# The first block pass begun on the first head pair, batch 1's v load behind its k, and q's first rows as two transfers

## The chip, the cores and the metric

One core of a Trainium2 chip runs the kernel. The metric is the device time of one execution in microseconds (us). Before the change three runs gave 291.13, 292.02 and 292.19 us: a median of 292.02 us.

## The reference

Eight batches of eight heads, 576 rows of 64 elements, go through a linear attention. Its output, as 4608 tokens of 512 features, goes through two matmuls with a leaky ReLU between them.

```python
q_s = q - np.max(q, axis=-1, keepdims=True)       # softmax of each q row
q_s = np.exp(q_s)
q_s = q_s / (np.sum(q_s, axis=-1, keepdims=True) + 1e-09)
k_s = k - np.max(k, axis=2, keepdims=True)        # softmax of k over the rows
k_s = np.exp(k_s)
k_s = k_s / (np.sum(k_s, axis=2, keepdims=True) + 1e-09)
kv = np.einsum('bhsd,bhse->bhde', k_s, v)
attn = np.einsum('bhsd,bhde->bhse', q_s, kv)
x = attn.transpose(0, 2, 1, 3).reshape(4608, 512)
h = x @ w_in                                      # 512 x 2048
out = np.maximum(0.01 * h, h) @ w_out             # 2048 x 512
```

## The kernel before, in words

The order of each engine's instructions is the order in which the program writes them; nothing is rescheduled. Work of a later batch is put between the matmuls of an earlier token tile by hand: `at(t, u, ...)` hangs functions on unit `u` of token tile `t`, and `run(t, u)` calls them (lines 493 to 500). Tile 0 has units 0 to 31 for `layer1` (two halves of 256 tokens, 16 blocks each) and 32 to 47 for `layer2`.

**Layout.** A batch's q, k or v is one tile of 128 partitions x 4 x 9 x 64: a head has 64 partitions, so a partition half holds one of two heads, four such pairs lie side by side, and a partition holds nine rows. `load` (line 72) issues such a tile on SyncE's queue, cut into pieces by head pair and by row.

**The start, batch 0.** SyncE issues rows 0 to 3 of q (`RA`), k in two halves, v in two halves, and the other q rows (lines 91 to 98). Then, engine by engine:

- VectorE takes the maxima of the first q rows (`q_first`, line 236) and ScalarE makes 16 exps with sums from them (line 241). VectorE makes k's maxima (`k_tree`, line 163), which TensorE turns and spreads (lines 338 and 353), and subtracts them (`k_sub_ps`, line 364). ScalarE exponentiates k (`k_exp`, line 204) and casts v to bf16 (`v_cast`, line 214).
- TensorE multiplies k and v for two of the four head pairs (`kv_pair`, line 373). VectorE scales the product to `kd` (lines 384 and 389). TensorE transposes q (`q_transpose`, line 397), the result is copied out (`q_keep`, lines 413 and 415), and `attend` (lines 421 and 431) multiplies it with `kd` and writes `xT`, the input of `layer1`. Rows 4 and 5 (`R1`) and 6 to 8 (`R2`) of q follow by `q_max` (228), `q_sub` (259, on GpSimd), `q_exp` (267), `q_sum` (276 and 278) and `q_norm` (283).
- `wake` (line 327) are matmuls on zeros whose result nobody reads.

**The first block pass.** `layer1` multiplies one 128-column block `j` of `w_in` with four feature blocks of `xT`; `part` says which of the four. Blocks 0 to 7 are begun with the two feature blocks of the first `attend` (lines 654 to 658) in four PSUM banks and ended with the other two (line 669); blocks 8 to 15 are done in one go. The transposes of q's rows 4 to 8 hang on units 7 and 11, their `attend` on unit 13. The PSUM pool of these results has six banks.

**Weights.** GpSimd's queue loads them, casting fp32 to bf16. `load_w_in(j0, j1)` (line 130) is four transfers over blocks `j0` to `j1`: two groups of feature blocks, and for each the two partition halves. The calls are for blocks 0 to 7, 8 to 11 and 12 to 15, the first two behind a tiny copy into `gate` that waits for a piece of k (lines 519 and 545), the third behind GpSimd's subtraction of q rows 4 and 5. `w_out` comes in six transfers behind a third such copy, which waits for batch 1's k (line 581).

**Batch 1.** Its loads stand in SyncE's queue behind a transfer of 256 bytes into `held`, whose source is a piece of `w_in_sb`, so that they are issued only when that piece has landed:

```python
hold_sync(0, w_in_sb[0:1, 1, 11 * P : 12 * P])
st[1]["k"] = load(k, 1, "k_raw", [(H0, ALLR), (H1, ALLR)])
st[1]["q"] = load(q, 1, "q_raw", [(ALLH, ALLR)])
st[1]["v"] = load(v, 1, "v_raw", [(ALLH, ALLR)])
nc.gpsimd.tensor_copy(out=gate[:, 0:1], in_=st[1]["k"][:, 0, 0, 0:1])
```

Partition 0 of feature block 1 is written by the third of the four transfers of `load_w_in(8, 12)`. Batch 1's softmax work hangs on units 15, 31, 34, 39 and 43, and its `attend_x` on 47. From token tile 1 on the plan is not touched by the change.

Of the kernel before, what the change touches and what calls it, by code (L numbers as in the profile page):

```python
# [8 lines left out]
FP32 = mybir.dt.float32  # L9
# [11 lines left out]
R = 9  # L21
HL = 4
# [3 lines left out]
def kernel(  # L26
# [9 lines left out]
    nc = tc.nc  # L36
# [3 lines left out]
    B, H, S, D = q.shape  # L40
    C = H * D
    T = B * S
    Cm, F = moe_w_in.shape
# [3 lines left out]
    P = 128  # L47
    NB = C // P
    NF = F // P
# [19 lines left out]
    BANK_TAG = "bank2k"  # L69


    def load(src, b, name, cuts):

        t = raw_pool.tile([P, HL, R, D], FP32, name=name, tag="raw")
        flat = src[b].rearrange("h s d -> (h s d)").rearrange(
            "(hl p r d) -> p hl r d", hl=HL, p=P, r=R
        )
        for hs, rs in cuts:
            nc.sync.dma_start(
                out=t[:, hs, rs].rearrange("p h r d -> p h (r d)"),  # L80
                in_=flat[:, hs, rs].rearrange("p h r d -> p h (r d)"),
            )
        return t

    ALLH, ALLR = slice(0, HL), slice(0, R)
# [2 lines left out]
    st = [{} for _ in range(B)]  # L88


    st[0]["q"] = load(q, 0, "q_raw", [(ALLH, RA)])
    st[0]["k"] = load(k, 0, "k_raw", [(slice(0, 2), ALLR), (slice(2, 4), ALLR)])
    st[0]["v"] = load(v, 0, "v_raw", [(slice(0, 2), ALLR), (slice(2, 4), ALLR)])
    qflat = q[0].rearrange("h s d -> (h s d)").rearrange("(hl p r d) -> p hl r d", hl=HL, p=P, r=R)
# [35 lines left out]
    def load_w_in(j0, j1):  # L130
        fs = slice(j0 * P, j1 * P)
        for gg in range(2):
            for hp in range(2):
                nc.gpsimd.dma_start(  # L134
                    out=w_in_t[hp * D : (hp + 1) * D, gg, :, fs], in_=w_in_r[gg, hp, :, :, fs]
                )
# [3 lines left out]
    def load_w_out(js):  # L140
        nc.gpsimd.dma_start(out=w_out_sb[:, js, :], in_=w_out_r[:, js, :])  # L141
# [61 lines left out]
    def k_exp(b, hs):  # L203
        nc.scalar.activation(  # L204
            out=st[b]["ke"][:, :, hs].rearrange("p r h d -> p h r d"),
            in_=st[b]["k"][:, hs],
            func=AF.Exp,
        )

    def v_cast(eng, b, gg):  # L210
        o = vb2[b % 2][:, :, gg, 0:128].rearrange("p r (h d) -> p h r d", h=2)
        i = st[b]["v"][:, 2 * gg : 2 * gg + 2]
        if eng is nc.scalar:
            eng.copy(out=o, in_=i)
        else:
            eng.tensor_copy(out=o, in_=i)  # L216
# [8 lines left out]
    def q_max(b, rs):  # L225
        n = rs.stop - rs.start
        st[b]["qmax", rs.start] = m = small_pool.tile([P, HL, n], FP32, name="qmax")
        nc.vector.tensor_reduce(out=m, in_=st[b]["q"][:, :, rs], axis=AX.X, op=ALU.max)  # L228
# [27 lines left out]
    def q_sub(eng, b, rs):  # L256
        n = rs.stop - rs.start
        qs = st[b]["q"][:, :, rs]
        eng.tensor_tensor(  # L259
            out=qs,  # L260
            in0=qs,
            in1=st[b]["qmax", rs.start].unsqueeze(3).to_broadcast([P, HL, n, D]),
            op=ALU.subtract,
        )

    def q_exp(b, rs):
        nc.scalar.activation(  # L267
            out=st[b]["qe"][:, rs].rearrange("p r h d -> p h r d"),
            in_=st[b]["q"][:, :, rs],
            func=AF.Exp,  # L270
        )

    def q_sum(b, rs):
        n = rs.stop - rs.start
        qsum = small_pool.tile([P, n, HL], FP32, name="qsum")
        nc.vector.reduce_sum(out=qsum, in_=st[b]["qe"][:, rs], axis=AX.X)  # L276
        st[b]["qrec", rs.start] = qrec = small_pool.tile([P, n, HL], FP32, name="qrec")
        nc.vector.reciprocal(out=qrec, in_=qsum)
# [46 lines left out]
    def wake(n):  # L325
        for i in range(n):
            nc.tensor.matmul(  # L327
                wake_ps, lhsT=zero[:, 0:P], rhs=zero, start=(i == 0), stop=(i == n - 1)
            )
# [16 lines left out]
    def k_all_dve(b, i):  # L346
        st[b]["kr", i] = kr = small_pool.tile([P, 2], FP32, name="kr")
        nc.vector.tensor_reduce(out=kr, in_=st[b]["kT", i], axis=AX.X, op=ALU.max)
# [19 lines left out]
    def kv_pair(b, gg):  # L368
        pkv = [psB_pool.tile([P, 130], FP32, name="pkv1", tag=BANK_TAG) for _ in range(2)]
        for r in range(R):  # L370
            for hh in range(2):
                rows = slice(hh * L, (hh + 1) * L)
                nc.tensor.matmul(
                    pkv[hh][:, 0:129],
                    lhsT=st[b]["ke"][rows, r, 2 * gg : 2 * gg + 2].rearrange("p h d -> p (h d)"),
                    rhs=vb2[b % 2][rows, r, gg, 0:129],
                    start=(r == 0),
                    stop=(r == R - 1),
                )
        st[b]["pkv", gg] = pkv  # L380
# [28 lines left out]
    def q_keep(eng, b, r0, n, ggs=(0, 1)):  # L409
        for gg in ggs:  # L410
            o, i = st[b]["qT", gg][:, :, r0 : r0 + n], st[b]["ps", r0][:, gg::2]
            if eng is nc.scalar:
                eng.copy(out=o, in_=i)
            else:
                eng.tensor_copy(out=o, in_=i)
# [77 lines left out]
    def at(t, u, *fns):  # L493
        while t > 0 and u >= 32:
            t, u = t + 1, u - 32
        hooks.setdefault((t, u), []).extend(fns)
# [11 lines left out]
        st[b]["v"] = load(v, b, "v_raw", whole)  # L508

    held = const_pool.tile([1, 2, 128], BF16)  # L510
    XR = (slice(0, 5), slice(5, R))

    def hold_sync(i, src):
        nc.sync.dma_start(out=held[:, i], in_=src)  # L514
# [19 lines left out]
    wake(1)  # L534
    k_sub_ps(0, 0, HA)
    k_exp(0, slice(0, 1))
    k_all_dve(0, 1)
    k_all_pe(0, 1)
    wake(5)
    k_sub_ps(0, 0, HB)  # L540
    k_exp(0, slice(1, 2))
    v_cast(nc.scalar, 0, 0)
    v_cast(nc.scalar, 0, 1)
    k_sub_ps(0, 1)
    nc.gpsimd.tensor_copy(out=gate[:, 0:1], in_=st[0]["k"][:, HL - 1, R - 1, D - 1 : D])  # L545
    load_w_in(8, 12)
    k_exp(0, slice(2, 3))
    q_first_rec(0, RA)
    q_norm(0, RA)
    kv_pair(0, 0)  # L550
    wake(1)
    q_transpose(0, 0, 4)
    wake(2)
    for hh in range(2):
        kd_rec(0, 0, hh)
        kd_one(nc.vector, 0, 0, hh)
    q_keep(nc.scalar, 0, 0, 4, (0,))
    k_exp(0, slice(3, 4))
    attend(0, [0, 2], 0, 256, nc.scalar)
    wake(1)  # L560
    kv_pair(0, 1)
    q_max(0, R1)
    q_sub(nc.gpsimd, 0, R1)
    load_w_in(12, 16)
    q_keep(nc.vector, 0, 0, 4, (1,))
    q_max(0, R2)
    q_sub(nc.gpsimd, 0, R2)
    kd_rec(0, 1, 0)
    kd_rec(0, 1, 1)
    kd_one(nc.vector, 0, 1, 0)  # L570
    kd_one(nc.vector, 0, 1, 1)
    q_exp(0, R1)
    q_sum(0, R1)
    q_norm(0, R1)


    hold_sync(0, w_in_sb[0:1, 1, 11 * P : 12 * P])
    st[1]["k"] = load(k, 1, "k_raw", [(H0, ALLR), (H1, ALLR)])
    st[1]["q"] = load(q, 1, "q_raw", [(ALLH, ALLR)])
    st[1]["v"] = load(v, 1, "v_raw", [(ALLH, ALLR)])  # L580
    nc.gpsimd.tensor_copy(out=gate[:, 0:1], in_=st[1]["k"][:, 0, 0, 0:1])  # L581
    for j0, j1 in ((0, 2), (2, 4), (4, 6), (6, 8), (8, 12), (12, 16)):
        load_w_out(slice(j0, j1))


    at(0, 7, lambda: q_transpose(0, 4, 2), lambda: q_keep(nc.vector, 0, 4, 2))
    at(0, 11, lambda: q_transpose(0, 6, 3), lambda: q_keep(nc.vector, 0, 6, 3))
    at(0, 13, lambda: attend(0, [0, 2], 256, 256, nc.scalar))
    at(0, 13, lambda: attend(0, [1, 3], 256, 256, nc.vector))
    at(0, 17, lambda: attend(0, [0, 2, 1, 3], 512, 64, nc.scalar))  # L590
    at(0, 15, lambda: k_begin(1), lambda: q_begin(1), lambda: k_tree(1, H0), lambda: k_tree(1, H1))
    at(0, 15, lambda: q_max(1, XR[0]), lambda: q_sub(nc.gpsimd, 1, XR[0]), lambda: k_allmax(1))
    at(0, 15, lambda: k_sub(nc.vector, 1, H0), lambda: k_sub(nc.vector, 1, H1))
    at(0, 15, lambda: q_max(1, XR[1]), lambda: q_sub(nc.gpsimd, 1, XR[1]))
    at(0, 31, lambda: q_exp(1, XR[0]), lambda: k_exp(1, H0), lambda: v_cast(nc.scalar, 1, 0))
    at(0, 31, lambda: k_exp(1, H1), lambda: v_cast(nc.scalar, 1, 1), lambda: q_exp(1, XR[1]))
    at(0, 31, lambda: q_sum(1, XR[0]), lambda: q_norm(1, XR[0]))
    at(0, 34, lambda: q_turn(1, XR[0]))
    at(0, 39, lambda: kv(1), lambda: q_sum(1, XR[1]), lambda: q_norm(1, XR[1]), lambda: kd_make(1))
    at(0, 43, lambda: q_turn(1, XR[1]), lambda: load_all(2))  # L600
    for i in range(8):
        eng = nc.vector if i in (5, 7) else nc.scalar
# [48 lines left out]

    g_sb = g_tiles()
    begun = []
    for j in range(0, 8, 2):
        ph = psB_pool.tile([P, 2, 256], FP32, name="ph", tag=BANK_TAG)
        for i in range(2):
            layer1(j + i, ph[:, i], 0, 256, slice(0, 2), i == 0)
        begun.append(ph)
        if j == 2:
            attend(0, [1, 3], 0, 256, nc.scalar)  # L660
    q_exp(0, R2)
# [1 line left out]
    q_norm(0, R2)  # L663
    for half in range(2):
        for j in range(0, NF, 2):
            part = slice(2, 4) if begun else slice(0, 4)
            ph = begun.pop(0) if begun else psB_pool.tile([P, 2, 256], FP32, name="ph", tag=BANK_TAG)
            for i in range(2):
                layer1(j + i, ph[:, i], 256 * half, 256, part, i == 0, i == 1)
                if i == 1:  # L670
                    leaky(g_sb[j // 2][:, :, 256 * half : 256 * half + 256], ph)
                run(0, 16 * half + j + i)
# [66 lines left out]
```

## Time and profile before

| What | Value |
| --- | --- |
| median of three runs | 292.02 us (291.13 to 292.19) |
| the profiled execution | 291.21 us |
| its span, first to last instruction | 289.4 us |
| granted TensorE clock | 1.000 |
| TensorE matmul busy | 279.8 us (97%) |
| VectorE, ScalarE, GpSimd busy | 149.5, 147.5, 84.8 us |
| `layer1` matmuls (L461), `layer2` matmuls (L482) | 127.5 us, 130.1 us |
| first `layer1` matmul, first `layer2` matmul | 16.71 us, 33.48 us |
| `wake` matmuls (L327) | 29, 9.3 us |

Line numbers are those of the kernel before. The page cuts the span into 40 slices of 7.2 us; a digit is the busy share in tenths:

```profile
PE   7689999999999999999999999999999999999995
...
DMA  7999999986839274953397239913141310131023
```

TensorE falls below nine tenths only in the first three slices and in the last. The DMA engines are at nine tenths or more in slices 2 to 8, from 7 to 58 us.

The landings of the early transfers, worked out from each one's start and its time to landing:

| Transfer | issued at, us | landed after, us |
| --- | --- | --- |
| q rows 0 to 3 (512 KB) | 0.74 | 3.9 |
| k, two halves | 1.26, 1.78 | 4.9, 5.9 |
| v, two halves | 2.29, 2.79 | 6.9, 7.9 |
| q rows 4 to 8 | 3.32 | 9.5 |
| `w_in` 0 to 7, four | 7.98 to 9.97 | 6.0, 6.2, 6.9, 7.5 |
| `w_in` 8 to 11, four | 12.91 to 14.6 | 5.2, 5.3, 5.3, 5.4 |
| `w_in` 12 to 15, four | 16.74 to 18.5 | 5.0, 4.7, 4.8, 5.1 |
| batch 1: k, two halves | 20.09, 20.67 | 4.8, 5.9 |
| batch 1: q, v | 21.24, 21.75 | 8.5, 13.4 |
| `w_out`, six | 25.43 to 29.1 | 8.0, 9.6, 10.1, 10.7, 12.5, 14.4 |

### The profile page before, as it was taken

What the parts mean: (1) busy time and instruction counts of PE and PEld (TensorE: products, weight loads), DVE (VectorE), ACT (ScalarE), POOL (GpSimd) and SP (SyncE); (2) the same over time, 40 slices, a digit from 0 to 9 for tenths busy, and PEclk for the clock granted to TensorE, in tenths of its full rate; (3) what the DMA queues carried; (4) which work ended last, traced back from release to release, by engine and by line L of the source; (5) the groups of instructions that cost most, each with busy time, mean ns of one, the idle gap of its engine ahead of it and who ended that gap; (6) DMA issues with size and microseconds to landing.
All of it is one profiled execution on the core that took longest, in us unless ns stands there. A gap on an engine that the chain in (4) does not pass through costs nothing.

```text
span 289.4 us, 4259 instructions
## 1 busy us (share of the span) xinstructions
PE 279.8 (97%) x1647; PEld 138.1 (48%) x1647; DVE 149.5 (52%) x245; ACT 147.5 (51%) x267; POOL 84.8 (29%) x65
## 2 busy tenths in 40 slices
PE   7689999999999999999999999999999999999995
PEld 2268654445444544454454444444455444444443
DVE  3998992986780894388175637654631200110011
ACT  4957761676269307922774348433853066016400
POOL 4675420026059009504900590039100000000000
PEclk9999999999999999999999999999999999999999
DMA  7999999986839274953397239913141310131023
GB/s 256 313 200 350 273 195 266 393 299 229 171 77 396 75 154 113 397 137 76 76 374 196 48 80 344 245 36 73 39 82 36 75 36 1 36 82 29 0 56 91
DMA packets 39508, 46.35 MB, mean 160 GB/s; under 512 B 18368, under 2 KB 22720, under 8 KB 39488
## 3 DMA queue, kind: packets, MB, share of 16 engines
q1 hardware_dynamic: 35456, 41.75, 48.7%
q0 software_dynamic: 3872, 4.20, 8.6%
q8 instruction: 13, 0.21, 0.3%
q10 hardware_dynamic: 160, 0.13, 0.1%
q14 instruction: 7, 0.06, 0.0%
HBM read 36.70 MB, written 9.44 MB: 159 GB/s over the span
## 4 chain that ended last, share of the span: by engine, by line
PE 86%; DMA 7%; DVE 1%; POOL 1%; ACT 1%; issue 0%; SPq 0%; POOLq 0%
PE pout L482 43%; PE ph L461 38%; DMA w_out_sb<-in_moe_w_out_dram 3%; PE pkv L298 3%; PE po L449 2%; DMA w_in_sb<-in_moe_w_in_dram 2%; DMA k_raw<-in_k_dram 2%; DVE k_raw L364 1%; ACT xT L455 1%; POOL w_in_sb L134 0%; POOL w_out_sb L141 0%; SPq L514 0%; DVE out_sb L476 0%; POOL gate L581 0%; POOL gate L545 0%
## 5 line engine op out<-in xcount | busy, mean ns | idle before, releaser
L482 PE MATMUL pout<-w_out_sb,gj 128*128 128x512 bf16 (+2 forms) x592 | 130.1, 374 | 0.4 <-DMA w_out_sb<-in_moe_w_out_dram 0.4
L461 PE MATMUL ph<-xT,w_in_sb 128*128 128x512 bf16 (+1 forms) x640 | 127.5, 358 | 0.1
L470 ACT ACTIVATE gj<-ph 128x512 bf16<-128x512 f32 x144 | 82.1, 604 | 56.3 <-PE ph L461 55.7
L461 PEld LDWEIGHTS <-w_in_sb 128*128 128x128 bf16 x640 | 62.2, 98 | 61.6 <-issue 0.6
L482 PEld LDWEIGHTS <-gj 128*128 128x128 bf16 x592 | 57.0, 98 | 63.1 <-issue 0.7
L476 DVE COPY out_sb<-pout 128x512 f32<-128x512 f32 (+1 forms) x34 | 22.7, 675 | 86.3 <-PE pout L482 80.8
L196 POOL TENSOR_TENSOR k_raw<-k_raw,kall 128x2304 f32<-128x2304 f32 x5 | 25.3, 5064 | 77.8 <-DVE kall L188 63.6
L455 ACT CAST xT<-po 128x320 bf16<-128x320 f32 (+1 forms) x54 | 18.8, 405 | 48.8 <-PE po L449 48.8
L259 POOL TENSOR_TENSOR q_raw<-q_raw,qmax 128x2304 f32<-128x2304 f32 (+4 forms) x11 | 31.2, 2844 | 29.8 <-DVE qmax L228 29.8
L276 DVE TENSOR_REDUCE qsum<-qe 128x36 f32<-128x2304 bf16 (+4 forms) x11 | 19.8, 1798 | 31.4 <-ACT qe L267 31.4
L283 DVE TENSOR_TENSOR qe<-qe,qrec 128x2304 bf16<-128x2304 bf16 (+4 forms) x12 | 23.9, 1989 | 0.4
L204 ACT ACTIVATE ke<-k_raw 128x2304 bf16<-128x2304 f32 (+2 forms) x12 | 17.8, 1479 | 9.9 <-POOL k_raw L196 8.6
L228 DVE TENSOR_REDUCE qmax<-q_raw 128x36 f32<-128x2304 f32 (+4 forms) x11 | 19.6, 1789 | 0.0
L267 ACT ACTIVATE qe<-q_raw 128x2304 bf16<-128x2304 f32 (+4 forms) x11 | 16.8, 1531 | 2.4 <-POOL q_raw L259 2.4
L216 POOL CAST vb<-v_raw 128x1152 bf16<-128x1152 f32 x12 | 13.4, 1150 | 0.0
L449 PE MATMUL po<-qX,kd 128*128 128x320 bf16 (+1 forms) x56 | 11.6, 286 | 0.3
L327 PE MATMUL pout<-zero 128*128 128x512 bf16 x29 | 9.3, 443 | 1.3 <-POOL zero L101 1.3
L163 DVE TENSOR_TENSOR t<-k_raw 128x1024 f32<-128x1024 f32 (+1 forms) x10 | 10.1, 1011 | 0.5 <-DMA k_raw<-in_k_dram 0.2
L476 ACT COPY out_sb<-pout 128x512 f32<-128x512 f32 (+1 forms) x3 | 1.7, 562 | 16.2 <-PE pout L482 16.2
L163 DVE TENSOR_TENSOR t<-t 128x256 f32<-128x256 f32 (+2 forms) x20 | 9.6, 478 | 0.7
L449 PEld LDWEIGHTS <-kd 128*128 128x128 bf16 x56 | 5.5, 98 | 6.8 <-issue 0.8
L298 PEld LDWEIGHTS <-ke 64*128 64x128 bf16 x252 | 7.1, 93 | 3.0 <-ACT gj L470 1.7
(58 smaller groups left out, 102.4 us busy)
## 6 DMA issues: line engine op xcount, KB each, us to landing
out_dram<-out_sb SPq DMA_DIRECT2D x70, 128.0 KB, 2.4
q_raw<-in_q_dram SPq DMA_DIRECT2D x7, 1152.0 KB, 8.5
v_raw<-in_v_dram SPq DMA_DIRECT2D x7, 1152.0 KB, 11.8
k_raw<-in_k_dram SPq DMA_DIRECT2D x6, 1152.0 KB, 5.7
k_raw<-in_k_dram SPq DMA_DIRECT2D x4, 576.0 KB, 5.4
v_raw<-in_v_dram SPq DMA_DIRECT2D x2, 576.0 KB, 7.4
w_in_sb<-in_moe_w_in_dram POOLq DMA_DIRECT2D x4, 256.0 KB, 6.5
w_in_sb<-in_moe_w_in_dram POOLq DMA_DIRECT2D x8, 128.0 KB, 5.1
```

Source lines behind the costliest of these rows:

```text
L163: nc.vector.tensor_tensor(out=o, in0=i0, in1=i1, op=ALU.max)
L196: eng.tensor_tensor(out=ks, in0=ks, in1=st[b]["kall"][:, hs].unsqueeze(2).to_broadcast([P, n, R, D]), op=ALU.subtract,)
L228: nc.vector.tensor_reduce(out=m, in_=st[b]["q"][:, :, rs], axis=AX.X, op=ALU.max)
L259: eng.tensor_tensor(out=qs, in0=qs, in1=st[b]["qmax", rs.start].unsqueeze(3).to_broadcast([P, HL, n, D]), op=ALU.subtract,)
L276: nc.vector.reduce_sum(out=qsum, in_=st[b]["qe"][:, rs], axis=AX.X)
L283: nc.vector.tensor_tensor(out=qes, in0=qes, in1=st[b]["qrec", rs.start].unsqueeze(3).to_broadcast([P, n, HL, D]), op=ALU.mult,)
L449: nc.tensor.matmul(ps.rearrange("p (r l) -> p r l", l=L), lhsT=kd2[b % 2][:, g], rhs=qX[:, gg, hh, rs])
L455: eng.copy(out=o, in_=ps)
L461: nc.tensor.matmul(ph, lhsT=w_in_sb[:, cb, j * P : (j + 1) * P], rhs=xT[:, XB[cb], c0 : c0 + n], start=(i == 0 and first), stop=(i == NB - ...
L470: nc.scalar.activation(out=o, in_=ph, func=AF.Prelu, alpha=LEAKY_SLOPE)
L476: copy(out=out_sb, in_=pout)
L482: nc.tensor.matmul(pout, lhsT=g_sb[j // 2][:, j % 2, tsub * P : (tsub + 1) * P], rhs=w_out_sb[:, j, os], start=(j == 0), stop=(j == NF - 1),)
```

## The change

It alters the order of the first 50 us and little else:

- q's first rows are loaded as two transfers, by head pairs 0 and 1 and 2 and 3; the second is issued by ScalarE's queue.
- The cast of v's second half goes from ScalarE to GpSimd, behind a new gate copy that waits for the first subtraction of k. Two exps of k's second half become one.
- `w_in` blocks 8 to 15 are loaded by one call of four transfers in place of two calls of four. The held transfer now reads partition 64 of feature block 0, which the second of the four writes.
- The second `kv_pair` stands in front of the first `attend`; one `wake` matmul fewer.
- The subtraction of q rows 6 to 8 goes from GpSimd to VectorE, behind the second pair's `kd`.
- A new transfer into `heldf` reads the last row of batch 1's k; v's load stands behind it in SyncE's queue, and both behind q's.
- In the first half of the first pass, blocks 8 to 15 are begun with two feature blocks as blocks 0 to 7 were, and q's rows 4 to 8 are transposed after that, in place of at units 7 and 11. Their `attend` goes from unit 13 to 11.
- Batch 1's casts of v come behind both exps of k, and its kv one unit later.

```diff
-    def load(src, b, name, cuts):
+    def load(src, b, name, cuts, queues=None):
...
-        for hs, rs in cuts:
-            nc.sync.dma_start(
+        for i, (hs, rs) in enumerate(cuts):
+            (queues[i] if queues else nc.sync).dma_start(
...
-    st[0]["q"] = load(q, 0, "q_raw", [(ALLH, RA)])
+    st[0]["q"] = load(
+        q, 0, "q_raw", [(slice(0, 2), RA), (slice(2, 4), RA)], (nc.sync, nc.scalar)
+    )
...
+    heldf = const_pool.tile([1, D], FP32)
...
     k_exp(0, slice(0, 1))
+    nc.gpsimd.tensor_copy(out=gate[:, 0:1], in_=st[0]["k"][:, 0, R - 1, D - 1 : D])
+    v_cast(nc.gpsimd, 0, 1)
...
     v_cast(nc.scalar, 0, 0)
-    v_cast(nc.scalar, 0, 1)
     k_sub_ps(0, 1)
     nc.gpsimd.tensor_copy(out=gate[:, 0:1], in_=st[0]["k"][:, HL - 1, R - 1, D - 1 : D])
-    load_w_in(8, 12)
-    k_exp(0, slice(2, 3))
+    load_w_in(8, 16)
+    k_exp(0, H1)
...
     q_transpose(0, 0, 4)
-    wake(2)
+    kv_pair(0, 1)
...
-    k_exp(0, slice(3, 4))
     attend(0, [0, 2], 0, 256, nc.scalar)
-    wake(1)
-    kv_pair(0, 1)
+    wake(2)
     q_max(0, R1)
     q_sub(nc.gpsimd, 0, R1)
-    load_w_in(12, 16)
     q_keep(nc.vector, 0, 0, 4, (1,))
-    q_max(0, R2)
-    q_sub(nc.gpsimd, 0, R2)
...
     q_exp(0, R1)
+    q_max(0, R2)
+    q_sub(nc.vector, 0, R2)
...
-    hold_sync(0, w_in_sb[0:1, 1, 11 * P : 12 * P])
+    hold_sync(0, w_in_sb[D : D + 1, 0, F - 128 : F])
     st[1]["k"] = load(k, 1, "k_raw", [(H0, ALLR), (H1, ALLR)])
     st[1]["q"] = load(q, 1, "q_raw", [(ALLH, ALLR)])
-    st[1]["v"] = load(v, 1, "v_raw", [(ALLH, ALLR)])
...
         load_w_out(slice(j0, j1))
+    nc.sync.dma_start(out=heldf, in_=st[1]["k"][0:1, HL - 1, R - 1])
+    st[1]["v"] = load(v, 1, "v_raw", [(ALLH, ALLR)])
...
-    at(0, 7, lambda: q_transpose(0, 4, 2), lambda: q_keep(nc.vector, 0, 4, 2))
-    at(0, 11, lambda: q_transpose(0, 6, 3), lambda: q_keep(nc.vector, 0, 6, 3))
-    at(0, 13, lambda: attend(0, [0, 2], 256, 256, nc.scalar))
-    at(0, 13, lambda: attend(0, [1, 3], 256, 256, nc.vector))
+    at(0, 11, lambda: attend(0, [0, 2], 256, 256, nc.scalar))
+    at(0, 11, lambda: attend(0, [1, 3], 256, 256, nc.vector))
...
-    at(0, 31, lambda: q_exp(1, XR[0]), lambda: k_exp(1, H0), lambda: v_cast(nc.scalar, 1, 0))
-    at(0, 31, lambda: k_exp(1, H1), lambda: v_cast(nc.scalar, 1, 1), lambda: q_exp(1, XR[1]))
+    at(0, 31, lambda: q_exp(1, XR[0]), lambda: k_exp(1, H0), lambda: k_exp(1, H1))
+    at(0, 31, lambda: v_cast(nc.scalar, 1, 0), lambda: v_cast(nc.scalar, 1, 1), lambda: q_exp(1, XR[1]))
...
-    at(0, 39, lambda: kv(1), lambda: q_sum(1, XR[1]), lambda: q_norm(1, XR[1]), lambda: kd_make(1))
+    at(0, 40, lambda: kv(1), lambda: q_sum(1, XR[1]), lambda: q_norm(1, XR[1]), lambda: kd_make(1))
...
-    for j in range(0, 8, 2):
+
+    def begin(j):
         ph = psB_pool.tile([P, 2, 256], FP32, name="ph", tag=BANK_TAG)
         for i in range(2):
             layer1(j + i, ph[:, i], 0, 256, slice(0, 2), i == 0)
         begun.append(ph)
+
+    for j in range(0, 8, 2):
+        begin(j)
...
         for j in range(0, NF, 2):
+            if half == 0 and j == 8:
+                for jj in range(8, NF, 2):
+                    begin(jj)
+                q_transpose(0, 4, 2)
+                q_transpose(0, 6, 3)
+                q_keep(nc.vector, 0, 4, 2)
+                q_keep(nc.vector, 0, 6, 3)
             part = slice(2, 4) if begun else slice(0, 4)
```

## The prediction

> **What bounds the kernel now.** I read the chain of waits first, from 12 us on. It names the first 36 us as a chain of transfers, not of matmuls (columns: start, length, what):
>
> ```profile
> 14.07 5.34 DMA w_in_sb<-in_moe_w_in_dram
> ...
> 19.42 0.63 SPq L514
> ...
> 20.09 4.76 DMA k_raw<-in_k_dram
> ...
> 25.43 0.74 POOL w_out_sb L141
> 26.17 9.57 DMA w_out_sb<-in_moe_w_out_dram
> ...
> 35.78 0.38 PE pout L482
> ```
>
> Read it backwards. TensorE's second pair of `w_out` blocks starts at 35.78 because the second `w_out` transfer landed then. That transfer was issued behind the gate on batch 1's k, k behind the held transfer on SyncE, and the held transfer behind the third transfer of `w_in` blocks 8 to 11. After 35.78 the chain is TensorE nearly to the end.
>
> Next the waits of TensorE between 15 and 50 us (total, times, longest):
>
> ```profile
> PE psum_qt L397 <- DVE qe L283: 1.1, 2, 0.7
> PE pout L482 <- DMA w_out_sb<-in_moe_w_out_dram: 0.4, 1, 0.4
> ```
>
> Only 1.5 us is idle, and 1.1 of it is in front of the transposes. The timelines of VectorE and GpSimd (start, length) show why:
>
> ```profile
> 12.93 1.23 DVE L283 TENSOR_TENSOR qe<-qe,qrec 128x1024 bf16<-128x1024 bf16 x1
> ...
> 18.48 2.73 DVE L283 TENSOR_TENSOR qe<-qe,qrec 128x512 bf16<-128x512 bf16 x1
> ```
> ```profile
> 19.13 1.53 POOL L259 TENSOR_TENSOR q_raw<-q_raw,qmax 128x768 f32<-128x768 f32 x1
> ```
>
> Half the elements took 2.73 us instead of 1.23, and the product ended 0.55 us after GpSimd's subtraction did (20.66).
>
> Last, the busy time by stretches: the stretch (length first), then PE, PEld, DVE, ACT and POOL, then the clock, the share of the DMA engines and GB/s.
>
> ```profile
> 20.00:22.00 2.00, 1.32 (x15) 0.97 (x13) 1.65 (x2) 1.31 (x3) 0.66 (x1) 1.00 1.22 190
> 28.00:30.00 2.00, 2.00 (x21) 1.79 (x20) 1.86 (x6) 1.50 (x4) 1.84 (x3) 1.00 1.05 378
> 36.00:38.00 2.00, 2.00 (x11) 0.94 (x10) 2.00 (x3) 2.00 (x3) 0.55 (x1) 1.00 1.24 207
> ```
>
> The DMA engines are full in all three. Their bytes are counted as written: GpSimd's queue shows 4.20 MB for 8.39 MB of weights read, so 205 GB/s of weights is 410 GB/s read. The stretch up to 36 us is therefore a stream of bytes in a fixed order. A gain on TensorE inside it shows only if `w_out` comes sooner.
>
> **TensorE's order, and what covers the gain.** Between 16.70 and 33.50 TensorE is busy 15.70 of 16.80 us. The first pass now has 16 matmuls of blocks 8 to 15 (16 x 0.112 = 1.8 us; 56 take 6.28) in front of the transposes. They need rows 6 to 8 of q normalised. On VectorE I count from the copy that ends at 16.0: two kd blocks 0.85, maximum 0.94, the subtraction of 768 elements 0.95 (between L364's 0.75 for 576 and L196's 1.35 for 1152), sum and reciprocal 0.88, product 0.68, sum and reciprocal 1.2, product 0.96. That is 22.4 us, and TensorE arrives at 20.5 + 1.8 = 22.3. The idle 1.1 us goes. `layer2` could start at 16.7 + 15.7 = 32.4 instead of 33.48. But the first `w_out` transfer, issued at 25.43, took 8.0 us and landed at 33.4, and the second at 35.75. TensorE would wait at the first and again at the second. The value is **0**, covered by the `w_out` stream; without that cover it is -1.1, and with the wait of 0.4 gone too -1.5.
>
> The same slack of 1 us covers small new waits: block 8 needs the second `w_in` transfer (20.0, needed 20.5), the halves of blocks 8 to 15 need the fourth (22.7 to 23.2, needed 22.9), and one PSUM bank returns 0.2 us late at the pulled-up `attend`.
>
> **ScalarE, GpSimd.** ScalarE loses one cast (1.14) and one exp's overhead (2 x 0.68 to 1.16). The copy of `psum_qt` behind them started at 14.87 because the transposes ended at 14.83, behind the product that ended at 14.16, so `layer1` still begins at 16.7: **0**. The cast on GpSimd (1.15 by L216) runs from 10.7, when v's second half has landed (2.79 + 7.9), to 11.9. The gate behind it waits until 12.74 anyway, so `w_in` 8 to 15 is issued at 12.9 as before: **0**, bounds 0 to +1.15 if the cast and VectorE's subtraction L364 shut each other out. I take 0, since L364 takes one operand from PSUM, and VectorE's maximum of one operand ran beside GpSimd's subtraction at 15.92 in its ordinary 0.94 us. The Trainium skill (SBUF — State Buffer, section SBUF: two separate sides) says that a VectorE operation with two SBUF inputs and a GpSimd operation that reads SBUF exclude each other for a whole instruction. The 2.73 us above agrees; by the rule too the cast costs nothing here and the subtraction moved to VectorE ends the stall.
>
> **kv(1) one unit later.** Block 8's matmuls stand where kv stood (41.05); the fifth `w_out` transfer landed at 28.36 + 12.5 = 40.86. Cover 0.2 us; value 0, bounds 0 to +0.2.
>
> **The held transfer.** It waited for the third transfer of 128 KB: issued 14.07, landed 19.41. Now it waits for the second of 256 KB. The queue is in order and full: blocks 0 to 7 end at 17.5 (9.97 + 7.5), the four of 128 KB landed 0.6 us apart, so two of 256 KB end at 17.5 + 2 x 1.25 = 20.05. **+0.65** for every SyncE issue behind it.
>
> **Batch 1's k.** Before, it shared the engines with blocks 12 to 15, the last of which landed at 23.5. Now these end by about 22.7, so k's first half has less beside it. Bounds: -0.65 (only the order of bytes counts) to 0. The engines would have a short hole, since k's data came about 1.8 us after its issue at 20.09 (202 GB/s in the half microsecond from 21.5, 294 in that from 22.0); I take **-0.25**. The `w_out` gate opens 0.4 later.
>
> **v behind k.** k's second half landed at 26.6 (20.67 + 5.9), q at 29.7, v at 35.2. In its queue v came after q anyway. Hung on k it is issued at 26.6 + 0.4 + 0.63 = 27.6, and with k's 1.8 us it is ready at 29.4, when q ends. So it meets the first `w_out` bytes as before: **0**. Bounds: 0 to -1.5 (above), if v comes late enough to leave the engines to `w_out`. The tiny extra transfer holds up only v.
>
> **q as two transfers.** The same 512 KB. The engines moved 96 and 203 GB/s in the half microseconds from 2.0 and 2.5, and 352 from 3.0: a slow start worth at most 0.3 us if two queues fill it. Bounds -0.3 to 0; I take **-0.15**, and the full stream moves up by it. ScalarE's issue (0.45, as SyncE's) lies in its 3.17 us of idleness. The Trainium skill (DMA: Bandwidth & Descriptors, section Issuing engines are not separate DMA queues) says that a second issuing engine saves only the time of issuing, as all transfers share 16 engines. By that the term would be 0 and the sum +0.4.
>
> **Sum**: 0.65 - 0.25 - 0.15 + 0 = +0.25 us. The profiled execution took 291.21 (span 289.4), which gives 291.5. The median shown, 292.02, lies 0.8 above it, so I forecast **292.3**. With every bound at its lower end (-0.65, -0.3, -1.5) the sum is -1.8, or 290.2; with every one at its upper (+1.15, +0.2) it is +2.0, or 294.0.
>
> **Rivals.**
> (1) *v steps aside.* If v's data starts well after 29.5, `w_out` gets the engines alone: two transfers of 1.25 us (third to fourth landed 1.3 apart) from 29.5 plus 0.7 to land are there at 32.7. TensorE then runs through: -1.1 - 0.4, with -0.15 from the start: 290.4. For it: v's 1.18 MB took 5.5 us from 29.7 to 35.2, half the rate. Against: v's issue at 27.6 is early enough not to leave a gap. Chance 0.18.
> (2) *The held transfer waits longer, and the whole stream with it.* The four 256 KB transfers before took 6.0 to 7.5 us from issue. The second of the new ones is issued at 13.7; it decides as soon as it lands past 20.0 (6.3 us). At 7.5 it lands at 21.2, 1.8 after 19.41; k has then nothing beside it to win back, and less 0.15 the time is 293.7. Against: the growth 6.0 to 7.5 came with q, k and v still loading, which ended at 12.8. Chance 0.16.
> (3) *The change doesn't do what it says*: v behind k comes when it came before. That is part of the forecast itself, whose chance is 0.66.
>
> **How the numbers follow.** About 0.5% (1.46 us) is what a measurement here can tell from no change: below 290.6 is faster, above 293.5 slower. Rival 1 lies just past its bound (0.12 of its 0.18), rival 2 too (0.10 of 0.16), and the forecast leaks 0.05 to each side: faster 0.17, slower 0.15, same 0.68. The range, 290.4 to 293.6, reaches to both rivals and leaves out only the corners where several bounds are at their ends together.
>
> **What would show it.** Right: no idle before the transposes, but one of 0.5 to 1 us before the first `w_out` matmul, `layer2`'s third block at 35.5 to 36.5, SyncE's held transfer at about 20. The stall of 2.73 us at the second product is gone. Wrong: third block before 35, or v landing past 37 (rival 1); held transfer past 20.7 (rival 2); a stretched L364 or cast at 11 us (the cast term).

## The result and the profile after

The changed kernel takes 293.26 us (median of 19 runs, 292.01 to 294.01); the kernel before takes 291.93 us (19 runs beside them, 290.72 to 292.29). The ratio is 1.0053, 95% interval 1.0039 to 1.0067: slower by 1.3 us by the medians and by 1.5 us by the ratio, whose interval is 1.1 to 2.0 us. The profiled execution took 293.26 us with a span of 291.5 us (289.4 before) and a granted clock of 1.000.

The chain of waits of the changed kernel, from 12 to 45 us (start, length, what):

```profile
13.77 7.30 DMA w_in_sb<-in_moe_w_in_dram
...
21.09 0.62 SPq L517
...
21.76 3.87 DMA k_raw<-in_k_dram
...
26.39 2.81 POOL w_out_sb L143 x4
29.20 13.42 DMA w_out_sb<-in_moe_w_out_dram
...
42.67 1.02 PE pout L484 x4
```

It is the same chain as before, but every link is later: the held transfer is issued at 21.09 (19.42 before), batch 1's k at 21.76 (20.09), `w_out` from 26.33 (25.43). It now joins TensorE for the last time at the fifth `w_out` transfer, which landed at 42.62 (40.86 before); in the kernel before that was the second.

TensorE's waits between 15 and 50 us (total, times, longest):

```profile
PE pout L484 <- DMA w_out_sb<-in_moe_w_out_dram: 2.4, 3, 1.2
PE ph L463 <- DMA w_in_sb<-in_moe_w_in_dram: 0.9, 1, 0.9
```

The wait before the transposes is gone. In its place stand 0.9 us for `w_in` block 8 and 2.4 us for `w_out`, in three pieces of 0.55, 1.20 and 0.67 us. `layer2` starts 0.62 us sooner than before (32.86 against 33.48), and its 33rd matmul, which needs the fifth transfer, at 42.67. `attend_x` begins at 50.80 (49.10 before): 1.7 us later. TensorE's timeline in the changed kernel (start, length, and in brackets the wait in front), then the `attend_x` of the kernel before:

```profile
32.86 1.89 PE L484 MATMUL pout<-w_out_sb,gj 128*128 128x512 bf16 x8
35.30 1.89 PE L484 MATMUL pout<-w_out_sb,gj 128*128 128x512 bf16 x8 [0.55 <-DMA w_out_sb<-in_moe_w_out_dram]
38.39 3.61 PE L484 MATMUL pout<-w_out_sb,gj 128*128 128x512 bf16 x16 [1.20 <-DMA w_out_sb<-in_moe_w_out_dram]
42.67 1.02 PE L484 MATMUL pout<-w_out_sb,gj 128*128 128x512 bf16 x4 [0.67 <-DMA w_out_sb<-in_moe_w_out_dram]
...
50.80 2.07 PE L451 MATMUL po<-qX,kd 128*128 128x320 bf16 x8
```
```profile
49.10 2.07 PE L449 MATMUL po<-qX,kd 128*128 128x320 bf16 x8
```

The other 0.4 us of the longer span lies in the 240 us behind it, where the change alters nothing; executions of one kernel differ by more than that.

Where the time went shows in half microseconds (stretch, then the engines, then clock, DMA share and GB/s). First the kernel before, then the changed one:

```profile
22.00:22.50 0.50, 0.50 (x8) 0.44 (x6) 0.50 (x1) 0.50 (x3) 0.00 (x0) 1.00 1.26 294
22.50:23.00 0.50, 0.50 (x7) 0.46 (x5) 0.43 (x3) 0.50 (x3) 0.00 (x0) 1.00 0.97 342
23.00:23.50 0.50, 0.42 (x4) 0.13 (x2) 0.50 (x1) 0.50 (x2) 0.00 (x0) 1.00 1.03 401
```
```profile
22.00:22.50 0.50, 0.50 (x7) 0.46 (x5) 0.11 (x1) 0.00 (x0) 0.00 (x0) 1.00 0.24 38
22.50:23.00 0.50, 0.50 (x7) 0.44 (x6) 0.00 (x0) 0.00 (x0) 0.00 (x0) 1.00 0.31 27
23.00:23.50 0.50, 0.50 (x12) 0.50 (x10) 0.13 (x1) 0.00 (x0) 0.00 (x0) 1.00 0.46 78
```

The DMA engines are nearly empty for 1.5 us: they moved 72 KB (half of 38 + 27 + 78) where 519 KB were moved before. At the 400 GB/s or so that they move from 24.0 on (396 and 429 in the next two half microseconds), that is an estimated 1.1 us of the stream lost.

Two parts of the change did what it says. On VectorE the second product takes 0.69 us in place of 2.73, and the cast on GpSimd its ordinary 1.15 us:

```profile
19.30 0.69 DVE L285 TENSOR_TENSOR qe<-qe,qrec 128x512 bf16<-128x512 bf16 x1
```
```profile
10.68 1.15 POOL L218 CAST vb<-v_raw 128x1152 bf16<-128x1152 f32 x1
```

### The profile page after: what moved, and what is told of

It is laid out like the page before. It is cut to its first block, busy times and chain, and to the rows that moved or that the text cites. A ratio compares the mean times of both kernels' runs of the same rounds, so it can differ in the third digit from the quotient of the medians.

```text
span 291.5 us, 4256 instructions
## 1 busy us (share of the span) xinstructions
PE 280.4 (96%) x1646; PEld 138.7 (48%) x1646; DVE 148.5 (51%) x246; ACT 146.9 (50%) x265; POOL 82.7 (28%) x62
## 4 chain that ended last, share of the span: by engine, by line
PE 83%; DMA 8%; POOL 1%; DVE 1%; ACT 1%; issue 0%; SPq 0%; POOLq 0%
PE pout L484 40%; PE ph L463 38%; DMA w_out_sb<-in_moe_w_out_dram 5%; PE pkv L300 3%; DMA w_in_sb<-in_moe_w_in_dram 3%; PE po L451 2%; DMA k_raw<-in_k_dram 1%; POOL w_out_sb L143 1%; DVE k_raw L366 1%; ACT xT L457 1%; POOL gate L581 0%; SPq L517 0%; POOL w_in_sb L136 0%; DVE out_sb L478 0%; POOL gate L549 0%
## 5 line engine op out<-in xcount | busy, mean ns | idle before, releaser
L261 POOL TENSOR_TENSOR q_raw<-q_raw,qmax 128x2304 f32<-128x2304 f32 (+3 forms) x10 | 29.7, 2972 | 30.2 <-DVE qmax L230 30.2
L285 DVE TENSOR_TENSOR qe<-qe,qrec 128x2304 bf16<-128x2304 bf16 (+4 forms) x12 | 21.8, 1818 | 0.4
L218 POOL CAST vb<-v_raw 128x1152 bf16<-128x1152 f32 x13 | 14.6, 1147 | 0.0
```

Of the source, the lines that this page charges most:

```text
L261: eng.tensor_tensor(out=qs, in0=qs, in1=st[b]["qmax", rs.start].unsqueeze(3).to_broadcast([P, HL, n, D]), op=ALU.subtract,)
L285: nc.vector.tensor_tensor(out=qes, in0=qes, in1=st[b]["qrec", rs.start].unsqueeze(3).to_broadcast([P, n, HL, D]), op=ALU.mult,)
```

## The experiments

Each kernel was timed beside the kernel before on the same chip. Theory A: the held transfer is released so late that the DMA engines run empty before batch 1's k arrives, and the whole stream of `w_out` is late. Theory B: hanging v on k costs the time.

### Undoing one part

**e1, the held transfer on the first of the four transfers.**

```diff
-    hold_sync(0, w_in_sb[D : D + 1, 0, F - 128 : F])
+    hold_sync(0, w_in_sb[0:1, 0, F - 128 : F])
```

> The change whole, but the held transfer reads partition 0 of feature block 0, so that it waits for the first transfer of w_in blocks 8 to 15 (landed at 19.0 in the changed kernel) and no longer for the second (21.07). Theory A, the late release of batch 1's k empties the DMA engines between 22 and 23.5 and puts the whole stream of w_out late: k issued near 19.7, no empty stretch, w_out issued near 25, and 1.2 to 1.7 us off the changed kernel, so 291.6 to 292.1. Theory B, hanging v on k costs the time because v's data comes into the middle of w_out: at most 0.4 us off the changed kernel, 292.9 or more.

Measured: 291.94 us (before 292.14), ratio 0.9998 (0.9982 to 1.0014). One index takes the whole loss back. SyncE's timeline (start, length) and the first of the half microseconds above, in this kernel:

```profile
18.90 0.62 SPq L517 DMA_DIRECT2D held<-w_in_sb  x1
19.56 1.25 SPq L79 DMA_DIRECT2D k_raw<-in_k_dram  x2
```
```profile
22.00:22.50 0.50, 0.50 (x7) 0.45 (x5) 0.09 (x1) 0.00 (x0) 0.00 (x0) 1.00 1.11 357
```

k is issued 2.2 us sooner than in the changed kernel, the empty stretch is gone, and v still hangs on k. This speaks for A and against B.

**e2, v right behind q.**

```diff
+    st[1]["v"] = load(v, 1, "v_raw", [(ALLH, ALLR)])
...
-    nc.sync.dma_start(out=heldf, in_=st[1]["k"][0:1, HL - 1, R - 1])
-    st[1]["v"] = load(v, 1, "v_raw", [(ALLH, ALLR)])
```

> The change whole, but v of batch 1 is issued right behind q, without the tiny transfer that reads k. Theory A: still 1.0 to 1.3 us above the kernel before (the engines are as empty from 22 to 23.5), v lands near 37, w_out issued near 26.3. Theory B: about the time of the kernel before, 292.0 within 0.3.

Measured: 293.05 us, ratio 1.0044 (1.0019 to 1.0069). By the median the loss stays, against B. TensorE's wait for `w_out` is now one of 2.1 us in place of three pieces. The clock fell behind it in the profile: 4 of 12 executions had a mean granted clock of 0.992 to 0.994 and took 294.3 to 295.3 us; the other eight took 291.7 to 293.8, with a median of 292.7, only 0.6 us above the kernel before. Part of e2's loss is thus the clock, and e2 alone leaves open whether v's place adds to the loss when the release is late.

**e3, both.** The edits of e1 and e2 together.

> Both: held transfer behind the first transfer of w_in blocks 8 to 15, and v issued right behind q. If the DMA order explains all of the loss, the time is that of the kernel before or up to 0.5 us less (291.4 to 292.0), with TensorE waiting for w_out as before. If the time stays above 292.5, something on the engines costs it too.

Measured: 292.17 us, ratio 0.9999 (0.9977 to 1.0020). That is 0.03 us above the 292.14 of the kernel before, so the late release explains the loss. With an early release it makes no measurable difference whether v hangs on k (e1) or not (e3). One of e3's 12 executions had a lowered clock (0.994); it is the slowest, 294.29 us, and the one that was profiled.

**e4, the DMA order of before in the changed kernel.**

```diff
-    load_w_in(8, 16)
+    load_w_in(8, 12)
...
+    load_w_in(12, 16)
...
-    hold_sync(0, w_in_sb[D : D + 1, 0, F - 128 : F])
+    hold_sync(0, w_in_sb[0:1, 1, 11 * P : 12 * P])
```

v is right behind q here too.

> The change with the DMA order of before put back: w_in blocks 8 to 11 and 12 to 15 in two calls, the held transfer on the third transfer of the first, v right behind q. What is left of the change is q as two transfers, the moved casts and subtraction, and TensorE's order. The forecast's term for these was 0 to -0.15 us, since the gain on TensorE is covered by w_out: 291.7 to 292.0. A gain of over 0.8 us would say that the cover is thinner than I had it; a loss would say that TensorE's new order costs time by itself.

Measured: 292.06 us, ratio 1.0014 (0.9994 to 1.0035). TensorE's new order, the moved cast and subtraction and the split q win nothing by themselves:

```profile
PE pout L482 <- DMA w_out_sb<-in_moe_w_out_dram: 0.4, 1, 0.4
```
```profile
PE pout L484 <- DMA w_out_sb<-in_moe_w_out_dram: 1.3, 1, 1.3
PE ph L463 <- DMA w_in_sb<-in_moe_w_in_dram: 1.1, 1, 1.1
```

The first line is the kernel before, the other two are e4: the 1.1 us that TensorE no longer waits for the transposes is waited for weights.

### Doing one part alone

**e5, only the merged load and its held transfer, in the kernel before.**

```diff
-    load_w_in(8, 12)
+    load_w_in(8, 16)
...
-    load_w_in(12, 16)
...
-    hold_sync(0, w_in_sb[0:1, 1, 11 * P : 12 * P])
+    hold_sync(0, w_in_sb[D : D + 1, 0, F - 128 : F])
```

> The kernel before with only this of the change: one load of w_in blocks 8 to 15 in four transfers, and the held transfer behind the second of them. Theory A (the late release of batch 1's k is the loss): held transfer near 21, DMA engines nearly idle around 22.5, 1.2 to 1.7 us slower than before, so 293.2 to 293.8. If the rest of the change is needed for the loss: within 0.4 us of the kernel before.

Measured: 293.27 us (before 291.83), ratio 1.0036 (1.0016 to 1.0056). The median is where A put it, but the profile shows another way there. TensorE's waits, and its clock (third from the right) in two microseconds behind the wait:

```profile
PE ph L461 <- DMA w_in_sb<-in_moe_w_in_dram: 2.0, 1, 2.0
```
```profile
24.00:26.00 2.00, 2.00 (x15) 1.57 (x12) 0.00 (x0) 0.89 (x2) 0.18 (x1) 0.50 1.05 385
```

In the order of before, blocks 8 and 9 need all four big transfers at once; TensorE waits until the fourth lands at 23.0. Then it runs at half its clock. Nine of 12 executions had a mean clock of 0.992 to 0.994 and took 293.2 to 294.2; the three whose clock stayed up took 291.7 to 291.9, the time of the kernel before. The held transfer was issued at 20.31 here, 0.8 sooner than in the changed kernel and 0.9 later than before; in those three executions that delay cost nothing. So e5 does not show that the late release alone costs the time. It shows what beginning blocks 8 to 15 on the first head pair is good for: with it, only two of the big transfers are needed at block 8.

**e6, only a later held transfer, in the kernel before.**

```diff
-    hold_sync(0, w_in_sb[0:1, 1, 11 * P : 12 * P])
+    hold_sync(0, w_in_sb[0:1, 0, F - 128 : F])
```

> The kernel before with one edit: the held transfer reads partition 0 of feature block 0 in blocks 12 to 15, so that it waits for the first transfer of the third w_in call (landed at 21.7 in the kernel before) and not for the third of the second call (19.4). The transfers keep their sizes. Theory A: 1.2 to 2.0 us slower than before, by the same empty stretch behind w_in. If the size of the transfers and not the time of release is what costs: within 0.4 us of before.

Measured: 294.7 us, ratio 1.0082 (1.0053 to 1.0111): more than A expected. The held transfer was issued at 21.78, and the engines moved 16 and 1 GB/s in the half microseconds from 22.5 and 23.0. The late release, with the old sizes of transfers, is enough for the loss. The excess is the clock:

```profile
35.00:37.00 2.00, 1.08 (x4) 0.53 (x5) 2.00 (x2) 2.00 (x2) 0.00 (x0) 0.91 1.24 209
37.00:39.00 2.00, 2.00 (x7) 0.64 (x5) 2.00 (x3) 2.00 (x3) 0.50 (x1) 0.50 1.24 207
```

Three executions with a clock of 0.999 or more took 292.9 to 293.9; four with 0.992 to 0.994 took 294.7 to 295.2.

**e9, the late held transfer with matmuls in the wait.** e6 plus

```diff
+    wake(8)
     pout = [psO_pool.tile([P, O], FP32, name="pout") for _ in range(2)]
```

> The kernel before with the late held transfer (on the first transfer of w_in blocks 12 to 15), plus eight matmuls on zeros between layer1 and layer2 of token tile 0, whose result nobody reads. With the late hold TensorE waited 2.1 us in one piece for w_out and its granted clock then fell to 0.50 for some 3.5 us in four of seven executions. If the long wait lowers the clock, the eight matmuls (1.7 us) fill it: no execution with a mean clock of 0.994 or less, and the time is that of the late hold's undisturbed executions, 292.9 to 293.9. If the clock falls for another reason, executions at 294.7 and more stay.

Measured: 293.3 us (before 291.55; 292.9 to 293.6), ratio 1.0051 (1.0034 to 1.0068), and no execution below a clock of 0.998. TensorE's timeline (seven of the eight matmuls stand in the trace), and its clock:

```profile
34.29 1.67 PE L327 MATMUL pout<-zero 128*128 128x512 bf16 x7
36.08 7.07 PE L482 MATMUL pout<-w_out_sb,gj 128*128 128x512 bf16 x32
```
```profile
37.00:39.00 2.00, 2.00 (x11) 0.92 (x10) 2.00 (x3) 2.00 (x3) 0.28 (x1) 1.00 1.24 206
```

This separates two costs: a late release by itself is worth about 0.5%, and the fallen clock comes on top when TensorE waits some 2 us in one piece.

**e10, the changed kernel again,** for the clock beside each time.

> The changed kernel itself, for the clock of each execution, which the first comparison does not list. If all of its loss is the later stream of bytes, the mean clock is 0.998 or more in all executions and the time 1.2 to 1.6 us above the kernel before. If the lowered clock has a part in it, some executions show 0.995 or less and are those above 293.8.

Measured: 293.58 us (293.05 to 293.88, six runs), ratio 1.0059 (1.0039 to 1.0078), mean clocks 0.997 to 1.000; two of the six are at 0.997, just under the 0.998 expected. The 19 executions of the first comparison have 0.997 or more too. Against 291.55 that is 2.0 us by medians, above the 1.2 to 1.6 expected; the ratio's interval (0.39 to 0.78%) is 1.1 to 2.3 us. The fallen clock has no part in the changed kernel's loss. TensorE waits 2.4 us for `w_out` here, but in four pieces, the longest of 1.0 us, where e2 waited 2.1 us in one.

### The tiny transfer

**e8, a tiny transfer that waits for nothing,** in e1.

```diff
+    nc.sync.dma_start(out=heldf, in_=identf[0:1, 0:D])
+    st[1]["v"] = load(v, 1, "v_raw", [(ALLH, ALLR)])
...
-    nc.sync.dma_start(out=heldf, in_=st[1]["k"][0:1, HL - 1, R - 1])
-    st[1]["v"] = load(v, 1, "v_raw", [(ALLH, ALLR)])
```

> A look at the tiny transfer: the change with the held transfer behind the first w_in transfer, and the tiny transfer still between q and v in SyncE's queue, but reading a constant, so that it waits for nothing. If the tiny transfer itself holds v's data back (they began 4.4 us after v's issue in the changed kernel), v's data begin late here too and w_out's first transfer lands before 32. If only the late issue does, v's data follow q's at once and w_out's first transfer lands near 35, as with v issued right behind q.

One run of 292.01 us. v's data followed q's without a gap, and the first `w_out` transfer landed at 33.1 (25.7 + 7.4), between the two forecasts. The stretch behind q's end in e8, and in the changed kernel:

```profile
30.00:30.50 0.50, 0.50 (x7) 0.46 (x5) 0.50 (x1) 0.31 (x1) 0.13 (x1) 1.00 1.10 291
```
```profile
31.50:32.00 0.50, 0.50 (x7) 0.45 (x6) 0.50 (x1) 0.41 (x1) 0.00 (x0) 1.00 1.22 181
32.00:32.50 0.50, 0.50 (x7) 0.46 (x5) 0.50 (x2) 0.31 (x1) 0.03 (x1) 1.00 1.20 239
```

About 200 GB/s is `w_out` alone (counted as written), about 290 is `w_out` and v together. In the changed kernel v was issued at 27.72 and joined only after 32. So a tiny transfer that is issued early does not hold v back. In the changed kernel both were issued late, the tiny one at 27.16 (it took 6.0 us to land); e8 does not separate a late tiny transfer from a late v. Part of the 4.4 us from v's issue to its data is q, which stood ahead of both in SyncE's queue: in the changed kernel it landed at 30.8, and the rate fell from 336 GB/s to 125 at 29.5. From there to v's first data are some 2.5 us. In e1, which also hangs v on k, the stretch at about 200 GB/s is nearly as long, from 28.5 to 30.5.

### Tries at a faster kernel

**e7, v behind the second `w_out` transfer.** e1, with `heldf` in bf16 as `w_out_sb` is, and

```diff
-    nc.sync.dma_start(out=heldf, in_=st[1]["k"][0:1, HL - 1, R - 1])
+    nc.sync.dma_start(out=heldf, in_=w_out_sb[0:1, 3, 0:D])
...
-    at(0, 31, lambda: q_exp(1, XR[0]), lambda: k_exp(1, H0), lambda: k_exp(1, H1))
-    at(0, 31, lambda: v_cast(nc.scalar, 1, 0), lambda: v_cast(nc.scalar, 1, 1), lambda: q_exp(1, XR[1]))
+    at(0, 31, lambda: q_exp(1, XR[0]), lambda: k_exp(1, H0), lambda: k_exp(1, H1), lambda: q_exp(1, XR[1]))
+    at(0, 31, lambda: v_cast(nc.scalar, 1, 0), lambda: v_cast(nc.scalar, 1, 1))
...
-    at(0, 40, lambda: kv(1), lambda: q_sum(1, XR[1]), lambda: q_norm(1, XR[1]), lambda: kd_make(1))
-    at(0, 43, lambda: q_turn(1, XR[1]), lambda: load_all(2))
+    at(0, 40, lambda: q_sum(1, XR[1]), lambda: q_norm(1, XR[1]))
+    at(0, 43, lambda: kv(1), lambda: kd_make(1), lambda: q_turn(1, XR[1]), lambda: load_all(2))
```

> A try at a faster kernel: the change with the held transfer behind the first transfer of w_in blocks 8 to 15, and batch 1's v hung on the second w_out transfer in place of k, with kv(1) three units later and the second q exp of batch 1 in front of the casts of v. If bytes in front of w_out are what TensorE waits for, w_out's fifth transfer lands 2 us sooner, TensorE has no wait for w_out, and 0.6 to 1.2 us are won against the kernel before (290.9 to 291.5). If v then comes too late for the casts, kv(1) waits and the gain is lost: 292.0 or more.

Measured: 294.39 us (before 291.83), ratio 1.0076 (1.0040 to 1.0111). TensorE had no wait for `w_out` any more, but:

```profile
PE pkv L300 <- ACT vb L216: 2.1, 1, 2.1
```

v was issued at 34.36, landed at 45.3, and behind the wait of 2.1 us the clock fell as well. Four of the seven executions had a mean clock of 0.994 or less and took 294.4 to 295.5 us; the other three took 292.1 to 293.5.

**e11, v behind the first `w_out` transfer,** kv(1) at unit 42.

```diff
-    nc.sync.dma_start(out=heldf, in_=w_out_sb[0:1, 3, 0:D])
+    nc.sync.dma_start(out=heldf, in_=w_out_sb[0:1, 1, 0:D])
```

> The try at a faster kernel once more, with batch 1's v hung on the first w_out transfer and no longer the second, and kv(1) one unit earlier than in that try. v is issued near 31, its data begin 3.5 us later, it lands near 41, and its casts end near 43.2, when TensorE reaches kv(1). Then TensorE waits neither for w_out nor for v, and the time is 0.4 to 1.0 us below the kernel before. If v still comes late, TensorE waits at kv(1) and the time is 0.3 us or more above.

Measured: 292.35 us (before 291.55), ratio 1.0032 (1.0007 to 1.0057). v landed at 42.9, and kv(1) waited 1.7 us for its casts, in two pieces of 1.35 and 0.37 us.

**e12, the casts side by side, kv(1) at unit 44.** e11, and

```diff
-    at(0, 31, lambda: v_cast(nc.scalar, 1, 0), lambda: v_cast(nc.scalar, 1, 1))
+    at(0, 31, lambda: v_cast(nc.scalar, 1, 0), lambda: v_cast(nc.gpsimd, 1, 1))
```

> The last try at a faster kernel: v hung on the first w_out transfer as in the try before it, where TensorE waited 1.7 us for the casts of v, but with the second cast on GpSimd beside the first on ScalarE and kv(1) two units later. The casts end near 44, TensorE reaches kv(1) at 44.4, and it waits neither for w_out nor for v: attend_x begins near 48.5 (49.1 before), and the time is 0.3 to 0.7 us below the kernel before. If kd then comes too late for attend_x, or v still comes late, it is at or above the kernel before.

Measured: 291.69 us (before 291.92), ratio 0.9998 (0.9980 to 1.0017): no gain. The wait moved to the fifth `w_out` transfer, for which TensorE stood 1.6 us, with v's bytes in front of it. No version beat the kernel before.

## Why the prediction was right and where it was off

The forecast was 292.3 us, 0.25 above the kernel before, with a range of 290.4 to 293.6. The time, 293.26, lies inside the range and on the forecast side, but five to six times as far from the kernel before as the sum said, and 0.53% is a little past the 0.5% that I had put down as slower with 0.15 (the interval, 0.39 to 0.67%, lies on both sides of it). The mechanism was right in outline: a stream of bytes in a fixed order, a gain on TensorE that it covers, and a held transfer that releases it later. Two terms were mis-sized, and the second rival came closest to what happened: the range holds the time because it reached out to that rival, not because the sum was right. Two of my signs of being wrong came: the held transfer was issued past 20.7 (21.09), and v landed past 37 (27.72 + 12.1 = 39.8).

- **The held transfer (+0.65).** This is the step that failed. I let two 256 KB transfers end at the queue's mean spacing, at 20.05. The second landed at 21.07, 7.3 us after its issue; the queue's spacing was right for the first (13.18 + 5.8 = 19.0). The term measured +1.67. Rival 2 named the mechanism, its point (past 20.0) and 7.5 us as its price, which is nearly what came. The term is not the same in every profile. With the same four transfers put into the kernel before (e5), the second landed 6.6 us after its issue and the held transfer was 0.89 late; in e10 and e2 the second took 7.3 and 7.6 us, in e11 6.3 and in e7 8.4. Why it lands up to 2.1 us behind the first was not tried.
- **Batch 1's k (-0.25).** I foresaw both the smaller competition and a hole. k's first half took 3.87 us in place of 4.76, so the term measured -0.9 by itself. The hole was far larger than the "short" one I wrote, as the rates from 22.0 show. With the gate copy's 0.64 us (0.18 before), `w_out` was issued 0.9 us later.
- **v behind k (0).** With the early release the term holds by time: e1 and e3 are equal. With the late one it is open: the intervals of the changed kernel and e2 overlap, but e2's holds executions with a lowered clock, and its other eight have a median 0.6 us above the kernel before, where the changed kernel is 1.3 to 2.0 above. By mechanism the term does not hold. I had v's data ready at 29.4; they came after 32. In this stretch `w_out` had the engines, so its first two transfers landed at 32.4 and 35.3 (33.4 and 35.75 before), although they were issued later. Half of rival 1 thus came true, and v's bytes were then in front of the later transfers.
- **TensorE's order (0, covered).** Right, and e4 agrees, whose interval is -0.06 to +0.35%. The wait before the transposes went, as forecast, with the stall of the second product. `layer2`'s third block began at 35.30, just ahead of the 35.5 to 36.5 named. The wait of 0.5 to 1 us that I named before the first `w_out` matmul did not come: that transfer landed at 32.4, and `layer2` started at 32.86. The wait of 0.92 us for block 8 was not in the sum: I had 0.5 us of slack for the second `w_in` transfer, and its landing at 21.07 took that too.
- **The cast on GpSimd (0).** Right for the cast: 1.15 us, with L366 beside it at its ordinary lengths and the gate still waiting for L366. But the `w_in` call behind the gate began at 13.18 and not at 12.9: a pause of 0.27 us stands between the gate copy and the first issue. It is there in every profile that has the cast on GpSimd and in none of the four without it (the kernel before, e5, e6, e9); the profile names no cause.
- **q as two transfers (-0.15).** k's maxima began at 6.05 in place of 6.19, 0.14 sooner, and q's at 4.23 in place of 4.68. This part was not run alone.
- **kv(1) behind block 8 (0 to +0.2).** TensorE waited 0.67 us at block 8 for the fifth transfer, which kv would have covered in part. This was not run alone either.

## What to carry to other kernels

When the transfer engines are the limit, a gate in front of a load is a matter of lead time: its release must come at least as long before the last queued byte as the next load takes to bring its first, or the engines stand empty and everything behind is late. Here that took somewhat over 2 us from the issue of the held transfer: the rate rose again between 23.0 and 23.5 behind an issue at 21.09. A gain on a compute engine inside such a stretch is worth nothing until the bytes come sooner. If a wait must remain, one of 2 us brings the risk of a lowered clock (4 of 12 executions in e2), and waits in pieces, of up to 1.2 us in the changed kernel's two profiles, did not (none of its 25 executions). By the medians, 293.05 and 293.26 us, the pieces won nothing here.

## What the hardware showed that was not expected

**The clock falls behind waits of 2 us, in part of the executions.** In the profiles of e2, e3, e5, e6 and e7 one wait of TensorE lasted 2.0 to 2.1 us, and its granted clock was then 0.50 for about 3.4 us, which costs some 1.7 us by estimate (half of it, with TensorE busy). Judged by a mean clock of 0.995 or less, this happened in 4 of 7 executions of e6 and of e7, 4 of 12 of e2, 9 of 12 of e5 and 1 of 12 of e3. In the profiles with longest waits of 1.3 (e4 and e11) and 1.6 us (e12) the mean clock stayed at 0.999 or more, and in e7 it was still 1.00 behind an earlier wait of 1.7 us for `w_in`. But 1 of 12 executions of e4 and 2 of 12 of e11, whose waits were not recorded, had 0.992 and took 294.8 to 295.3 us. With matmuls in the wait (e9) it stayed up in all eight. The Trainium skill (TensorE: Matmul & The Clock Gate, section Why this matters for your kernels) says that gaps over some 3 us between bursts of matmuls bring the half rate. The half rate agrees with the 0.50 here, but gaps of 2.0 us were enough in part of the executions.

**A load issued late behind others took long to begin.** v's data began more than 4 us after its issue at 27.72 in the changed kernel, the last 2.5 us or so with `w_out` alone on the engines; k's, issued at 20.09 in the kernel before, after about 2. The first part is q, ahead of it in the queue. Why the rest is no shorter than for a load with nothing but the held transfer ahead of it is open; e8 rules out only a tiny transfer that is issued early.
